# phi(q) kept in DRAM with its 32-row blocks in their new order, and loaded in one transfer, for 22 of 32 tiles; new ranks for the list that orders the program

## The chip, the cores and the metric

One Trainium2 chip, one of its cores. The kernel runs alone on that core; the time is device time in microseconds (us) from launch to end, taken for each execution, and a version's time is the median of its runs.

## The reference

x has 2048 rows of 640 float32 numbers. Two equal layers are applied, each a linear attention block of 32 heads of 20 columns and an MLP with a squared ReLU of 1728 columns, with a layer norm before each and the input added to the output:

```python
def _A_ref(x, wqkv, wo):
    B, S, D = x.shape
    H = 32; Dh = D // H
    qkv = (x @ wqkv).reshape(B, S, 3, H, Dh).transpose(2, 0, 3, 1, 4)
    q, k, v = qkv[0], qkv[1], qkv[2]
    phi = lambda t: jnp.where(t > 0, t + 1, jnp.exp(t)) + 1e-6
    pq, pk = phi(q), phi(k)
    kv = jnp.einsum("bhsd,bhse->bhde", pk, v)
    z = jnp.einsum("bhsd->bhd", pk)
    num = jnp.einsum("bhqd,bhde->bhqe", pq, kv)
    den = jnp.einsum("bhqd,bhd->bhq", pq, z)[..., None] + 1e-6
    return (num / den).transpose(0, 2, 1, 3).reshape(B, S, D) @ wo
def _B_ref(x, w1, b1, w2, b2):
    h = jnp.einsum("bsd,df->bsf", x, w1) + b1
    r = jnp.where(h > 0, h, 0)
    return jnp.einsum("bsf,fd->bsd", r * r, w2) + b2
x = A_x
for layer in range(2):
    x = x + _A_ref(_layernorm(x), A_wqkv, A_wo)
    x = x + _B_ref(_layernorm(x), B_w1, B_b1, B_w2, B_b2)
```

## The kernel before

**Tiles and stages.** The rows are 16 tiles of 128 (t = 0 to 15), in four groups of four. Every float32 matrix product is made of three matmul passes, from operands that are split into a high and a low part. A layer has three stages. *Stage A* makes k and q of all tiles, phi of both, and gathers kv and z (the sum of phi(k)). phi(q) of a tile, 128 x 640, is written to a DRAM buffer `pqd[t]` by SP (L1075 and L1159), since kv is known only when all tiles are through. For six tiles of each layer, `LATE` (9, 11, 12, 13, 14, 15 in layer 0 and 8, 9, 11, 13, 14, 15 in layer 1), q is made later, in a *bridge* between the stages, and stored at L1190, the last of them (tile 15) at L2194 in `late_line`. The bridge makes M (kv times wo) and starts the first unit of the MLP. The *group stage* then runs the attention output and the MLP of the four groups, interleaved.

**phi(q) on its way back.** `b_load_pq` (L839) loads a tile as `pqt`. Its 4 x 4 blocks of 32 rows and 160 columns change places on the way, so that the later transposes of 32 x 32 blocks come out right: a tile comes in four transfers of 32 x 4 x 160 numbers (L842), each from pieces of 160 numbers (640 bytes) in DRAM. `b_ops` (L849) works on it on DVE in four steps: `pr` = pqt times z (L853), the sum per head `den` (L860), its reciprocal and pqt times it (L866, L867, L869), and the transpose to `z` (L874). `p_split` on ACT and DVE makes the matmul operand `pT` of it.

**Pairs.** Two tiles together get their attention output in seven products (class `Pair`: p1, p2, p4, p6, p7, p5, p3) on PE, which all use the PSUM bank `po0`. After each, ACT or DVE reads the bank, in DVE's case with the adds of L1913 (`uu`, `su`, `xr`), and only then can PE start the next product.

**MLP.** The first product goes by units in Strassen's manner (PE L1584, adds L1616 and L1626 on DVE), the second is PE L1733. Their weights are kept in DRAM as `kept_w...` and come through a ring of buffers `u` by SP's loads at L572, each of which waits until PE has freed a buffer.

**What sets the order.** The program is scheduled by hand: each engine runs its instructions in the order in which they were written. For the group stage a planner (classes `Line` and `Clock`) sets that order while the program is built. Generators, called lines (`q_line` with the load of pqt and b_ops, `pair_line`, `fc1_line`, `fc2_line`, `ring_line`, `late_line` and others), yield steps such as `"SP", cost, call`, and `Clock` keeps an estimated time for each engine. Of the lines whose next step could go on an engine, the one with the smallest key goes first: its time less `early`, then its rank. `RANK` (L60) holds a pair (rank, early) for each kind of line, layer and group, and `at`, the times at which ACT, DVE and other engines are taken to be free as the stage begins. In a step for SP a number is the cost of one transfer, and a tuple that of four (`n = 4 if isinstance(us, tuple) else 1`). SP's queue holds all loads and stores in one order; each waits there for its buffer or its data.

Of the kernel before, what the change touches and what calls it, by code (L numbers as in the profile page):

```python
# [23 lines left out]
B32 = 32  # L24
# [34 lines left out]

RANK = (  # L60
    dict(
        full=((4, 0.0), (5, 0.0), (4, 0.0), (9, 0.4)),
        half=((5, 0.8), (5, 0.8), (5, 0.8), (5, 0.8)),
        moves=((8, 0.0), (4, 0.0), (5, 0.8), (9, 0.2)),
        unit=((2, 0.0), (2, 0.0), (2, 0.2), (0, -0.5)),
        next=((5, 0.8), (5, 0.8), (5, 0.8), (5, 0.8)),
        preset=((1, 0.0), (0, 0.8), (2, 0.2), (2, 0.2)),
        strip=((9, 0.0), (9, -0.2), (2, -0.2), (2, -0.2)),
        bias=((4, 0.0), (3, 0.2), (3, 0.2), (3, 0.0)),
        fc1=((4, -0.2), (1, -0.2), (1, -0.2), (2, -0.2)),  # L70
        fc2=((6, 0.0), (8, 0.0), (6, 0.0), (6, 0.0)),
        q0=((5, 0.0), (5, 0.0), (3, 0.0), (2, 0.8)),
        q1=((6, 0.0), (6, 0.0), (6, 0.0), (2, 0.0)),
        pair=((2, 0.0), (0, 0.0), (0, -0.2), (0, 0.2)),
        load_x=((5, 0.0), (5, 0.0), (5, 0.0), (5, 0.0)),
        x0=((5, 0.0), (9, 0.0), (9, -0.5), (9, -0.5)),
        x1=((9, 0.0), (4, 0.0), (4, 0.0), (4, 0.0)),
        t=((1, 0.2), (2, 0.2), (5, 0.4), (4, 0.0)),
        x1_load=((9, -0.2), (6, -0.2), (6, -0.2), (6, -0.2)),
        late=((4, 0.8), (4, 0.8), (9, 0.8), (9, 0.8)),  # L80
        mixed=((0, 0.4), (8, 0.4), (0, 1.5), (6, 1.5)),
        ring=((0, 0.0), (2, 1.5), (7, 1.5), (0, 0.0)),
        kq=((3, 0.4), (3, 0.0), (4, 0.0), (3, 0.0)),
        at=(5.0, 5.6, 2.2, 13.3),
    ),
    dict(
        full=((0, 0.0), (0, 0.0), (0, 0.8), (0, -0.5)),
        half=((6, 0.2), (1, 0.0), (1, 0.0), (1, 0.0)),
        moves=((3, 0.0), (1, 0.8), (6, 0.8), (9, 0.0)),
        unit=((1, 0.8), (1, 0.8), (1, 0.8), (1, 1.5)),  # L90
        next=((4, -0.2), (5, -0.2), (5, -0.2), (5, 0.0)),
        preset=((7, 0.0), (9, 0.0), (1, 0.0), (4, 0.0)),
        strip=((8, 0.0), (8, 0.0), (8, 0.0), (8, 0.0)),
        bias=((9, -0.2), (8, -0.5), (2, -0.5), (3, 0.0)),
        fc1=((5, 0.0), (0, 0.0), (3, 0.0), (2, 0.0)),
        fc2=((6, 0.4), (3, 0.4), (3, 0.4), (7, 0.4)),
        q0=((9, 0.0), (2, 0.0), (0, 0.0), (4, 0.0)),
        q1=((6, 0.0), (6, 0.0), (6, 0.0), (2, 0.0)),
        pair=((0, 0.0), (2, 0.0), (2, 0.0), (4, 0.0)),
        load_x=((7, 0.4), (7, 0.4), (7, 0.4), (7, 0.4)),  # L100
        x0=((5, 0.0), (9, 0.2), (3, 0.0), (5, 0.0)),
        x1=((9, 0.0), (6, 0.0), (8, -0.2), (8, -0.2)),
        t=((7, -0.5), (7, -0.2), (2, -0.2), (1, 0.4)),
        x1_load=((0, 0.4), (0, 0.4), (0, 0.4), (0, 0.4)),
        late=((9, 0.2), (2, 0.2), (2, 0.4), (0, 0.0)),
        mixed=((3, 0.0), (9, 0.0), (0, 0.0), (0, 0.0)),
        ring=((2, 0.0), (2, 0.0), (7, 0.0), (2, 0.0)),
        kq=((5, -0.5), (5, -0.5), (5, -0.5), (5, 0.4)),
        at=(4.8, 3.8, 1.5, 19.7),
    ),  # L110
)
T_FIRST = "0 u0 2 0 v0 2 u0 2 u2 v0 2 v2 u2 v2"
# [179 lines left out]
def kernel(  # L292
# [405 lines left out]
    for layer in range(N_LAYERS):  # L698
# [138 lines left out]
        def b_load_pq(t):  # L837
            if t < NT:
                pq[t] = ftile("pqt")  # L839
                v = pqd[t].rearrange("(i q) (j r) -> j q i r", i=JB, j=JB)  # L840
                for j in range(JB):
                    nc.sync.dma_start(  # L842
                        pq[t][j * B32 : (j + 1) * B32].rearrange("q (i r) -> q i r", i=JB), v[j]
                    )

        def b_load_x(t):
            xr[t] = ftile("xr")
# [123 lines left out]
        for t in range(NT):  # L971
# [15 lines left out]
            if first:  # L987
# [197 lines left out]
        def late_rest(n=9):  # L1185
            for _ in range(min(n, len(late_todo))):
                t, j = late_todo.pop(0)
                late_phi[t].rest()
                if j == 1:
                    nc.sync.dma_start(pqd[t], late_phi.pop(t).r)  # L1190

        late_q(1)
        if layer == 0:
# [785 lines left out]
        def q_line(t, first, after):  # L1979
# [209 lines left out]
        def late_line():  # L2189
            t = late_todo[-1][0]  # L2190
            for n in range(2):
                yield "DVE", 2 * cost("DVE", HD), lambda: late_phi[t].rest(1)
            yield "made", "late"
            yield "SP", MB, lambda: nc.sync.dma_start(pqd[t], late_phi[t].r)  # L2194
            yield "end f", 1
            yield "end f", 1, "got"

# [201 lines left out]
```

## Time and profile before

| what | us |
|---|---|
| median of three runs | 1330.86 |
| the runs | 1327.1, 1330.92, 1330.86 |
| the profiled execution | 1328.1 |
| span of the profiled execution | 1326.3 |
| PE busy | 1315.4 |
| DVE busy | 978.9 |
| ACT busy | 774.3 |

The page's times are those of one execution; the span runs from its first instruction to its last. An engine's busy time is the sum over its instructions. Transfers are listed by their issues: of the 128 loads of pqt (80 KB each) the median from issue to landing was 5.6 us, of the stores from stage A (320 KB) 2.3 us. A name such as "DVE pr L853 <- DMA pqt<-pq" in a list of waits reads: DVE, about to write pr at line 853, waited for the transfer that fills pqt from pq.

### The profile page before, as it was taken

The page shows a single profiled execution, that of the slowest core. Times are in us where ns is not written, and L with a number is a line of the kernel's source. Part 1 is how long each engine was busy: PE and PEld are TensorE (multiplying, and loading weights), DVE is VectorE, ACT ScalarE, POOL GpSimd, SP SyncE. Part 2 cuts the span into 40 slices and gives each one's busy share as a digit, 9 for nine tenths or more (in the row PEclk, how much of TensorE's full clock was granted, in tenths as well). Part 3 has the DMA queues.
Part 4 walks back from the last instruction along what each step waited for, and adds up shares of the span by engine and source line. Part 5 has one row for each costly group of instructions (what it writes and reads, how often), then busy time and mean ns, then how long its engine had stood idle before and what let it go on. Part 6 is the DMA issues. An engine that isn't in the chain of part 4 may idle for free.

```text
span 1326.3 us, 21333 instructions
## 1 busy us (share of the span) xinstructions
PE 1315.4 (99%) x7616; PEld 1177.2 (89%) x7616; DVE 978.9 (74%) x1923; ACT 774.3 (58%) x1760; POOL 145.5 (11%) x194
## 2 busy tenths in 40 slices
PE   9999999999999999999999999999999999999999
PEld 8888899989889889888888899998998898898887
DVE  8989988899887786552467678799978887765323
ACT  5988865745665645642757687557364744654422
POOL 1343410000000000000112132000000000000000
PEclk9999999999999999999999999999999999999999
DMA  6679876496878868799821114276877888687775
GB/s 209 226 273 342 319 241 190 146 331 218 284 256 325 282 206 295 264 351 360 276 100 42 59 40 126 58 213 202 283 254 237 281 299 271 222 297 262 275 284 177
DMA packets 118656, 310.86 MB, mean 234 GB/s; under 512 B 14934, under 2 KB 40150, under 8 KB 118518
## 3 DMA queue, kind: packets, MB, share of 16 engines
q1 hardware_dynamic: 117038, 306.81, 67.9%
q10 hardware_dynamic: 1512, 2.69, 0.7%
q8 instruction: 60, 0.98, 0.3%
q14 instruction: 46, 0.38, 0.1%
HBM read 248.66 MB, written 62.23 MB: 234 GB/s over the span
## 4 chain that ended last, share of the span: by engine, by line
PE 93%; DVE 3%; DMA 2%; ACT 1%; issue 1%; POOL 0%; SPq 0%; DVEq 0%; ACTq 0%; POOLq 0%
PE PS L643 35%; PE PS L1733 27%; PE PS L1584 17%; PE PS L1594 5%; PE PS L1550 3%; PE PS L664 3%; PE PS L1261 1%; PE PS L1290 1%; PE PS L997 1%; DMA pqt<-pq 1%; DMA st<-in_B_w_dram 1%; DMA u<-kept_wG 1%; DMA u<-kept_w 0%; ACT z L631 0%; PE PS L793 0%
## 5 line engine op out<-in xcount | busy, mean ns | idle before, releaser
L1733 PE MATMUL PS<-u,h 128*128 128x512 f32 x1318 | 342.2, 391 | 2.0 <-DMA u<-kept_w 2.0
L631 ACT ACTIVATE z<-y 32x160 f32<-32x160 f32 x774 | 258.5, 334 | 66.3 <-DVE y L618 55.5
L643 PE MATMUL PS<-kq,xT 128*128 128x320 f32 (+2 forms) x1575 | 282.1, 334 | 0.2 <-DVE GT L785 0.2
L1733 PEld LDWEIGHTS PS<-u,h 128*128 128x128 f32 x1318 | 238.9, 188 | 45.8 <-ACT uT L2202 1.7
L643 PEld LDWEIGHTS PS<-kq,xT 128*128 128x128 f32 x1575 | 250.2, 188 | 25.7 <-issue 1.0
L1584 PE MATMUL PS<-tx,u 128*128 128x256 f32 x1152 | 161.5, 283 | 1.0 <-ACT s L1606 0.8
L1584 PEld LDWEIGHTS PS<-tx,u 128*128 128x128 f32 x1152 | 151.0, 191 | 4.8 <-ACT s L1606 1.0
L1662 ACT ACTIVATE hr<-PS,b1sb 128x512 f32<-128x512 f32 x104 | 71.4, 686 | 127.4 <-PE PS L1594 103.2
L1584 PEld LDWEIGHTS PS<-xTb,u 128*128 128x128 f32 x864 | 121.4, 190 | 10.9 <-ACT PS L1612 1.0
L1584 PE MATMUL PS<-xTb,u 128*128 128x256 f32 x864 | 126.4, 282 | 0.5 <-ACT PS L1612 0.5
L598 POOL TENSOR_SCALAR rs<-mv 128x1 f32<-128x1 f32 x62 | 32.9, 531 | 847.7 <-DVE mv L595 847.7
L643 PE MATMUL PS<-kh,xh 128*128 128x512 f32 x480 | 124.5, 392 | 0.1
L1668 DVE TENSOR_TENSOR hr<-hr 128x512 f32<-128x512 f32 x73 | 49.8, 688 | 69.5 <-ACT h L1681 69.3
L643 PEld LDWEIGHTS PS<-kh,xh 128*128 128x128 f32 x480 | 87.0, 188 | 15.1 <-DVE kh L935 0.5
L746 ACT ACTIVATE e<-PS 128x320 f32<-128x320 f32 (+4 forms) x128 | 53.3, 435 | 76.9 <-PE PS L643 70.0
L1733 PE MATMUL PS<-h,u 128*128 128x512 f32 x328 | 93.2, 392 | 0.0
L1681 ACT ACTIVATE h<-hr 128x512 fp32r<-128x512 f32 x104 | 64.6, 629 | 38.2 <-PE PS L1733 36.7
L1594 PE MATMUL PS<-xTb,u 128*128 128x512 f32 x288 | 79.1, 393 | 0.0
L754 DVE TENSOR_SCALAR e<-e 128x320 f32<-128x320 f32 (+4 forms) x128 | 41.7, 326 | 50.6 <-ACT e L746 50.3
L1671 DVE TENSOR_TENSOR h<-hr,h 128x512 fp32r<-128x512 f32 x104 | 70.5, 684 | 8.2 <-ACT hr L1666 5.4
L1733 PEld LDWEIGHTS PS<-h,u 128*128 128x128 f32 x328 | 59.8, 188 | 11.2 <-ACT h L1681 0.2
L1616 DVE TENSOR_TENSOR PS<-PS,s 128x256 f32<-128x256 f32 x48 | 20.8, 433 | 63.0 <-ACT PS L1612 63.0
(172 smaller groups left out, 1906.2 us busy)
## 6 DMA issues: line engine op xcount, KB each, us to landing
u<-kept_w SPq DMA_DIRECT2D x116, 640.0 KB, 5.4
u<-kept_wE SPq DMA_DIRECT2D x48, 512.0 KB, 4.4
u<-kept_wH SPq DMA_DIRECT2D x48, 512.0 KB, 4.9
u<-kept_wG SPq DMA_DIRECT2D x48, 512.0 KB, 4.4
u<-kept_wF SPq DMA_DIRECT2D x48, 512.0 KB, 5.4
x<-x SPq DMA_DIRECT2D x40, 320.0 KB, 5.4
pqt<-pq SPq DMA_DIRECT2D x128, 80.0 KB, 5.6
st<-in_B_w_dram SPq DMA_DIRECT2D x26, 320.0 KB, 4.9
```

The lines of the kernel that those rows point to most:

```text
L631: nc.scalar.activation(d, v, AF.Copy)
L643: nc.tensor.matmul(ps, a, b, start=first and i == 0, stop=last and i == 2)
L664: nc.tensor.matmul(ps[:, j * 512 : j * 512 + HD], aT[:, k, c, :], w[c][:, l, j * HD : (j + 1) * HD], start=c == 0 and i == 0, stop=c == DC ...
L746: nc.scalar.activation(self.e[:, a:b], ps, AF.Exp)
L754: nc.vector.tensor_scalar(e, e, 1.0, PHI_EPS, op0=ALU.min, op1=ALU.add)
L1584: nc.tensor.matmul(ps, l[:, d], r[:, d], start=start and d == 0 and n == 0, stop=d == 1 and n == 2, skip_group_check=True,)
L1594: nc.tensor.matmul(ps, l[:, k], r, start=False, stop=n == 2, skip_group_check=True)
L1662: nc.scalar.activation(r, ps, AF.Relu, bias=b1sb[:, c : c + 1])
L1668: nc.vector.tensor_tensor(out=r, in0=r, in1=r, op=ALU.mult)
L1671: nc.vector.tensor_tensor(out=h[:, 1], in0=r, in1=h[:, 0].bitcast(F32), op=ALU.subtract)
L1681: yield "ACT", cost("ACT", GT), lambda: nc.scalar.activation(h[:, 0], r, AF.Square)
L1733: nc.tensor.matmul(ps, l, r, start=(first or new) and k == 0, stop=end and k == len(a) - 1, **loose)
```

## The change

A function `stored_turned(t)` is true for all tiles of layer 1 and for the six late tiles of layer 0, 22 of 32. Such a tile is written to DRAM with its blocks already in the new order, in four stores (`q_store`), and comes back in one load of 128 x 640. The other ten tiles are stored in one transfer and loaded in four, as before. The planner is told so: the load of a turned tile costs one transfer, the store of `late_line` four. The rank tables of both layers are replaced.

```diff
@@ RANK, layer 0 (two of its 23 rows)
-        pair=((2, 0.0), (0, 0.0), (0, -0.2), (0, 0.2)),
+        pair=((1, 0.0), (3, 0.0), (1, 0.0), (1, 0.0)),
...
-        at=(5.0, 5.6, 2.2, 13.3),
+        at=(4.8, 5.1, 2.9, 13.8),
@@ def b_load_pq(t):
             if t < NT:
                 pq[t] = ftile("pqt")
+                if stored_turned(t):
+                    nc.sync.dma_start(pq[t], pqd[t])
+                    return
                 v = pqd[t].rearrange("(i q) (j r) -> j q i r", i=JB, j=JB)
                 for j in range(JB):
                     nc.sync.dma_start(
                         pq[t][j * B32 : (j + 1) * B32].rearrange("q (i r) -> q i r", i=JB), v[j]
                     )
 
+        def stored_turned(t):
+            return layer > 0 or t in LATE[layer]
+
+        def q_store(t, r):
+
+            if not stored_turned(t):
+                nc.sync.dma_start(pqd[t], r)
+                return
+            v = pqd[t].rearrange("(j q) (i r) -> i q j r", i=JB, j=JB)
+            for i in range(JB):
+                nc.sync.dma_start(v[i], r[i * B32 : (i + 1) * B32].rearrange("q (j r) -> q j r", j=JB))
@@ stage A, tile 0
-                nc.sync.dma_start(pqd[0], fq.r)
+                q_store(0, fq.r)
@@ stage A, the other tiles
-                    nc.sync.dma_start(pqd[t], f.r)
+                    q_store(t, f.r)
@@ late q
-                    nc.sync.dma_start(pqd[t], late_phi.pop(t).r)
+                    q_store(t, late_phi.pop(t).r)
@@ def q_line(t, first, after):
-                yield "SP", (MB / 0.75,), lambda: b_load_pq(t)
+                yield "SP", MB if stored_turned(t) else (MB / 0.75,), lambda: b_load_pq(t)
@@ def late_line():
-            yield "SP", MB, lambda: nc.sync.dma_start(pqd[t], late_phi[t].r)
+            yield "SP", (MB / 0.75,), lambda: q_store(t, late_phi[t].r)
```

What lies behind the inserted functions has its line number raised by 15: L853 is now L868, L1913 is L1928, L1584 is L1599. A load of a turned tile is L841, its stores are L859, and a store in one transfer is L855.

The order of the instructions moves in the group stages. Three places follow. In the rows, a name with <- is a destination and its sources, and x4 means four such instructions in a row. The first is SP in the bridge of layer 1, where the late tiles 13 to 15 are stored (`rl`) and tile 5 is loaded. Before:

```order
L1190 DMA pq_13_7343<-rl 128x640
L1190 DMA pq_14_7344<-rl 128x640
L572 DMA u<-kept_wH_780 128x1024
L842 DMA pqt<-pq_5_7335 32x4x160 x4
L572 DMA u<-kept_wG_782 128x1024
L572 DMA u<-kept_wF_637 128x1024
L2194 DMA pq_15_7345<-rl 128x640
```

And SP at the same place with the change:

```order
L859 DMA pq_13_7343<-rl 32x4x160 x4
L859 DMA pq_14_7344<-rl 32x4x160 x4
L572 DMA u<-kept_wH_780 128x1024
L841 DMA pqt<-pq_5_7335 128x640
L572 DMA u<-kept_wG_782 128x1024
L572 DMA u<-kept_wF_637 128x1024
L859 DMA pq_15_7345<-rl 32x4x160 x4
```

The order is the same; three stores are four instructions each, the load is one.

The second place is DVE in layer 0, with the block of b_ops of one of the last tiles and the pair adds of tiles 12 and 13. Before:

```order
L853 TENSOR_TENSOR pr<-pqt,zbc 128x640
L860 TENSOR_REDUCE den<-pr 128x32
L866 TENSOR_SCALAR den<-den 128x32
L867 RECIPROCAL den<-den 128x32
L869 TENSOR_TENSOR pqt<-pqt,den 128x640
L874 STREAM_TRANSPOSE z<-pqt 128x640
L1913 TENSOR_TENSOR uu<-PS,uu 128x320
L1913 TENSOR_TENSOR xr<-uu,xr 128x640
```

DVE at that pair with the change:

```order
L1928 TENSOR_TENSOR xr<-PS,xr 128x320
L868 TENSOR_TENSOR pr<-pqt,zbc 128x640
L1928 TENSOR_TENSOR uu<-PS,su 128x320
L875 TENSOR_REDUCE den<-pr 128x32
L881 TENSOR_SCALAR den<-den 128x32
L882 RECIPROCAL den<-den 128x32
L884 TENSOR_TENSOR pqt<-pqt,den 128x640
L1683 TENSOR_TENSOR hr<-hr 128x512
L1768 STREAM_TRANSPOSE strip<-PS 128x512
L1631 TENSOR_TENSOR PS<-PS,s_5457 128x256
L1804 TENSOR_TENSOR x_4888<-PS,x_4888 128x512 x2
L1928 TENSOR_TENSOR uu<-PS,uu 128x320
```

The add of p6 (uu from PS and su) has moved into the block, and the add of p7 (uu from PS and uu) stands further behind it, with work of the MLP between.

The third place is the last pairs of layer 1. DVE there before, with the block of tile 15:

```order
L853 TENSOR_TENSOR pr<-pqt,zbc 128x640
L860 TENSOR_REDUCE den<-pr 128x32
L866 TENSOR_SCALAR den<-den 128x32
L867 RECIPROCAL den<-den 128x32
L869 TENSOR_TENSOR pqt<-pqt,den 128x640
L1913 TENSOR_TENSOR su<-PS,uu 128x320
L1913 TENSOR_TENSOR xr<-PS,xr 128x320
```

DVE with the change, the block of tile 15 and the first rows of that of tile 14, which is now the later one:

```order
L868 TENSOR_TENSOR pr<-pqt,zbc 128x640
L875 TENSOR_REDUCE den<-pr 128x32
L881 TENSOR_SCALAR den<-den 128x32
L882 RECIPROCAL den<-den 128x32
L884 TENSOR_TENSOR pqt<-pqt,den 128x640
L1641 TENSOR_TENSOR PS<-PS,s_12336 128x256
L889 STREAM_TRANSPOSE z<-pqt 128x640
L1928 TENSOR_TENSOR xr<-PS,xr 128x320
L1797 TENSOR_TENSOR x_11389<-sz,x_11389 128x4x128
L868 TENSOR_TENSOR pr<-pqt,zbc 128x640
L875 TENSOR_REDUCE den<-pr 128x32
L1928 TENSOR_TENSOR uu<-PS,su 128x320
```

An add of an MLP unit (L1641) and two pair adds now stand behind the blocks. On SP, tile 15's load stands right behind the load of `kept_wF_786`, which waits for a buffer.

PE at the same place with the change runs these from the matmuls that free that buffer, in a first part:

```order
L1748 MATMUL PS<-u,h 128x512 x6
L1748 MATMUL PS<-h,u 128x512 x2
L1748 MATMUL PS<-u,h 128x512 x3
L643 MATMUL PS<-uM,pT 128x320 x6
L1599 MATMUL PS<-xTb,u 128x256 x6
L1599 MATMUL PS<-tx,u 128x256 x6
L643 MATMUL PS<-uT_9874,pT 128x320 x6
```

The second part of PE's rows follows directly:

```order
L643 MATMUL PS<-uM,pT 128x320 x3
L1599 MATMUL PS<-tx,u 128x256 x6
L1748 MATMUL PS<-u,h 128x512 x6
L1599 MATMUL PS<-xTb,u 128x256 x6
L1599 MATMUL PS<-tx,u 128x256 x12
L1748 MATMUL PS<-u,h 128x512 x3
L1748 MATMUL PS<-h,u 128x512 x3
L1599 MATMUL PS<-xTb,u 128x256 x6
```

The last of these rows is the one that works on the result of L1641; the rows ahead of it are 23 matmuls of 512 columns, 15 of 320 and 36 of 256.

More of the change, by code (lines that the diff above doesn't have):

```diff
@@ L61 @@
     dict(
[L62 to L70, printed above, removed]
@@ L80 @@
[L80 to L83, printed above, removed]
-        at=(5.0, 5.6, 2.2, 13.3),
+        full=((5, 0.0), (3, 0.0), (4, 0.0), (8, 0.8)),
+        half=((3, 0.8), (5, 0.8), (6, -0.2), (9, -0.2)),
+        moves=((6, 0.0), (1, -0.2), (5, 0.8), (2, 0.0)),
+        unit=((3, 0.0), (3, 0.0), (6, 0.0), (6, 0.2)),
+        next=((5, 0.4), (2, -0.2), (5, 0.0), (2, 0.8)),
@@ L85 @@
+        x0=((5, 0.0), (7, 0.0), (9, -0.5), (8, -0.2)),
+        x1=((9, 0.0), (4, 0.0), (4, -0.2), (4, -0.2)),
+        t=((1, 0.2), (3, 0.4), (3, -0.2), (2, 0.2)),
+        x1_load=((9, 0.0), (9, 0.4), (4, -0.2), (4, -0.2)),
+        late=((5, 0.8), (5, -0.2), (5, -0.2), (5, -0.2)),
+        mixed=((7, 0.4), (8, -0.2), (6, 0.4), (6, 0.4)),
+        ring=((0, 0.2), (0, 0.2), (0, 0.2), (0, 0.2)),
+        kq=((3, 0.0), (3, 0.0), (0, 1.5), (3, 0.0)),
+        at=(4.8, 5.1, 2.9, 13.8),
     ),
     dict(
-        full=((0, 0.0), (0, 0.0), (0, 0.8), (0, -0.5)),
@@ L106 @@
[L106 to L109, printed above, removed]
+        full=((1, 0.0), (1, 0.0), (1, 0.0), (1, 0.0)),
+        half=((6, 0.2), (0, -0.2), (4, 0.0), (1, 0.0)),
+        moves=((7, 0.8), (3, 0.4), (2, 0.4), (2, 0.8)),
+        unit=((7, 0.0), (3, 0.8), (7, 0.0), (3, 0.0)),
+        next=((2, 0.0), (5, 0.0), (2, 0.0), (2, -0.5)),
+        preset=((5, 1.5), (5, 1.5), (5, 1.5), (5, 1.5)),
@@ new lines @@
+        strip=((1, 0.4), (8, 0.0), (4, 0.0), (6, 1.5)),
+        bias=((6, -0.2), (5, 0.8), (5, 0.8), (5, 0.8)),
+        fc1=((3, 0.0), (0, 0.0), (3, 0.0), (3, 0.0)),
+        fc2=((8, 1.5), (7, 0.0), (6, 0.0), (9, 0.2)),
+        q0=((9, 0.0), (1, 0.0), (9, 0.0), (9, 1.5)),
+        q1=((9, 0.0), (5, 1.5), (5, 1.5), (5, 1.5)),
+        pair=((5, 0.0), (5, 0.0), (0, 0.0), (0, 0.0)),
+        load_x=((0, 0.0), (5, 0.4), (5, 0.4), (5, 0.4)),
+        x0=((2, 0.0), (2, 0.0), (2, 0.0), (2, 0.0)),
@@ L110 @@
+        x1=((9, 0.0), (9, 0.0), (9, 0.0), (9, 0.0)),
+        t=((0, -0.5), (2, 1.5), (2, 1.5), (2, 1.5)),
+        x1_load=((2, 0.8), (7, 0.2), (7, 0.2), (7, 0.2)),
+        late=((9, 0.2), (1, 0.2), (1, 0.8), (1, 0.4)),
+        mixed=((6, 0.0), (6, 0.0), (6, 0.0), (6, 0.0)),
+        ring=((3, 0.0), (3, 0.0), (3, 0.0), (3, 0.0)),
+        kq=((0, 1.5), (9, -0.5), (7, -0.5), (7, 0.2)),
+        at=(4.8, 3.8, 0.0, 22.7),
     ),
```

34 lines of the change are left out of this document (8 added, 26 removed).

## The prediction

> **What bounds the kernel now.** I read the page's first lines first, then its summary of the chain that ended last.
>
> ```profile
> span 1326.3 us, 21333 instructions
> PE 1315.4 (99%) x7616; PEld 1177.2 (89%) x7616; DVE 978.9 (74%) x1923; ACT 774.3 (58%) x1760; POOL 145.5 (11%) x194
> PE 93%; DVE 3%; DMA 2%; ACT 1%; issue 1%; POOL 0%; SPq 0%; DVEq 0%; ACTq 0%; POOLq 0%
> ```
>
> TensorE is busy for 1315.4 of 1326.3 us. The change leaves the number of matmuls alone, so it can only win or lose time in which PE waits. Where that time lies is shown by busy time per stage (columns: window, length, then PE, PEld, DVE, ACT and POOL busy with counts, granted clock, DMA share, GB/s). The six windows are stage A of layer 0, its first unit, its group stage, then the same three of layer 1.
>
> ```profile
> 0.00:196.00 196.00, 193.65 (x1039) 170.21 (x1040) 172.44 (x335) 152.81 (x360) 63.48 (x78) 1.00 0.79 270
> 196.00:262.00 66.00, 64.67 (x449) 62.15 (x448) 57.27 (x118) 41.47 (x90) 4.03 (x8) 1.00 0.54 163
> 262.00:667.00 405.00, 403.84 (x2346) 359.91 (x2346) 282.66 (x555) 218.47 (x486) 17.50 (x33) 1.00 0.82 284
> 667.00:855.00 188.00, 188.00 (x1015) 166.04 (x1014) 137.53 (x270) 124.75 (x310) 43.72 (x43) 1.00 0.25 75
> 855.00:932.00 77.00, 74.97 (x499) 70.48 (x498) 68.50 (x137) 46.48 (x98) 4.03 (x8) 1.00 0.63 194
> 932.00:1326.30 394.30, 390.31 (x2279) 348.43 (x2277) 260.46 (x512) 190.30 (x420) 12.73 (x24) 1.00 0.76 261
> ```
>
> PE's idle time is 2.35, 1.33, 1.16, 0, 2.03 and 3.99 us. Little is left to take: in the two group stages, where the order changes, 1.16 us and, in the second, the 3.99 us with the tail after the last matmul in it. The clock was 1.00 throughout, so no stage is slow for that. Next, who ended PE's waits (total us, times, longest), and DVE's waits for the tensor that the change touches:
>
> ```profile
> PE PS L1733 <- DMA u<-kept_w: 2.0, 2, 1.5
> PE PS L643 <- DVE xr L1913: 0.9, 1, 0.9
> PE PS L643 <- DVE uu L1913: 0.9, 1, 0.9
> PE PS L1584 <- ACT s L1606: 0.8, 1, 0.8
> DVE pr L853 <- DMA pqt<-pq: 4.2, 4, 1.8
> ```
>
> PE never waits for pqt itself. DVE does, four times, and the two PE waits of 0.9 us for DVE's L1913 stand behind two of those. So the whole visible prize of a faster pqt load is some 1.8 us. The chance of a larger effect, either way, lies in the new rank tables.
>
> **Part 1: the load in one transfer.** Place A is tile 15 of layer 1. The rows are SP's four issues, the last piece's landing as the chain has it, DVE's product pr, its next add on the chain, and the matmul that waits:
>
> ```profile
> 1110.98 2.28 SPq L842 DMA_DIRECT2D pqt<-pq  x4
> 1112.76 8.16 DMA pqt<-pq
> 1121.04 0.82 DVE L853 TENSOR_TENSOR pr<-pqt,zbc 128x640 f32<-128x640 f32 x1 [1.35 <-DMA pqt<-pq]
> 1124.18 0.40 DVE su L1913
> 1124.58 0.41 DVE xr L1913
> 1125.04 1.59 PE L643 MATMUL PS<-uM,pT 128*128 128x320 f32 x9 [0.95 <-DVE xr L1913]
> ```
>
> The piece that lands last was issued 1112.76 − 1110.98 = 1.78 us after the first. One transfer is issued where the first piece was, so if it takes the same 8.16 us from issue to landing, DVE starts 1.35 us earlier (all of its wait, since 1.78 is more) and PE's 0.95 us go: **−0.95**, with 0.40 us of DVE's gain left over. From below: if one transfer of 320 KB takes 1.78 us longer than a piece of 80 KB, nothing is won (0).
>
> Place B is the same pair of tiles in layer 0, tiles 14 and 15, which are among the six turned there:
>
> ```profile
> 456.29 2.83 SPq L842 DMA_DIRECT2D pqt<-pq  x4
> 464.98 0.83 DVE L853 TENSOR_TENSOR pr<-pqt,zbc 128x640 f32<-128x640 f32 x1 [1.84 <-DMA pqt<-pq]
> 475.52 0.45 DVE L1913 TENSOR_TENSOR uu<-PS,uu 128x320 f32<-128x320 f32 x1
> 476.02 1.15 PE L643 MATMUL PS<-uT,uS 128*128 128x320 f32 x6 [0.86 <-DVE uu L1913]
> ```
>
> DVE lost 1.84 us at 464.98, worked without a further wait for a pqt, and came to uu too late by 0.86. In the new order one block of L868 to L884 stands ahead of this uu, with another pair add inside it. With four issues in 2.83 us there, one issue saves up to that; I take **−0.86**. From below 0, if the new order makes uu wait for something else.
>
> **Part 2: the new order at the same pair (C).** In layer 1's new order the block of tile 15 (L868 to L884) stands ahead of the add L1641, whose result a unit of the MLP's first product on PE needs, and SP issues that load right behind a weight load that waits for a free buffer. So the load cannot start early, and what DVE has queued behind pr waits with it: L1641, the transpose of z, a pair add and the block of tile 14. PE's rate comes from three long rows of the chain of waits, and a landing is known for pieces and for whole 320 KB tiles in the last stage:
>
> ```profile
> 655.97 10.88 PE PS L1733 x48
> 221.43 13.20 PE PS L664 x90
> 375.62 2.15 PE PS L1584 x18
> DMA to landing us min/median/max: 3.9/6.0/8.8
> x<-x SPq DMA_DIRECT2D x12, 320.0 KB, 5.4
> xr<-x SPq DMA_DIRECT2D x10, 320.0 KB, 6.2
> ```
>
> One matmul takes 10.88/48 = 0.227 us at 512 columns, 13.20/90 = 0.147 at 320, 2.15/18 = 0.119 at 256. From the matmul that frees the weight buffer to the one that needs L1641 the new order has 23, 15 and 36 of these: 5.21 + 2.20 + 4.30 = 11.7 us. Against that stands DVE's work after the landing, 1124.18 − 1121.04 = 3.14 us for the block plus some 0.4 for L1641 (it takes as long as su's 0.40), and some 0.5 us (my estimate from SP's single issues of 0.32 to 0.36 below) from the release to the issue. So the landing must come within 11.7 − 3.14 − 0.4 − 0.5 = 7.7 us of the issue. The median row says 6.0, the 320 KB rows 5.4 and 6.2, the worst piece 8.8: spare 1.5 to 2.3, or short by 1.1. I take **+0.4** (bounds 0 and 1.5, the latter from 1.1 plus 0.4 for the two pair adds that stand behind and have little spare either).
>
> The Trainium skill (DMA: Bandwidth & Descriptors, section "Anatomy of one DMA — SWDGE (gpsimd) path") gives a transfer a fixed 2.0 us or so plus its bytes over 436 GB/s; for 320 KB that is an estimate of 2.75 us, C would cost 0, and the whole sum would be 0.4 us lower. The trace differs: 5.4 and 6.2 us, with the transfer engines 0.76 busy in that stage, so the measurement decides.
>
> **Part 3: the bridge, where late tiles are stored (D).** A turned store is four issues instead of one, and SP is in order. In layer 1 the first unit of the MLP stands right behind:
>
> ```profile
> 898.47 6.23 SPq L1190 DMA_DIRECT2D pq<-rl  x2
> 904.81 0.36 SPq L572 DMA_DIRECT2D u<-kept_wH  x1
> 905.27 2.03 SPq L842 DMA_DIRECT2D pqt<-pq  x4
> 913.47 0.32 SPq L2194 DMA_DIRECT2D pq<-rl  x1
> 913.89 0.86 SPq L848 DMA_DIRECT2D xr<-x  x2
> 917.54 0.32 SPq L572 DMA_DIRECT2D u<-kept_w  x1
> 912.63 0.88 PE L1584 MATMUL PS<-tx,u 128*128 128x256 f32 x6
> u<-kept_wH SPq DMA_DIRECT2D x2, 512.0 KB, 4.2
> 922.79 2.14 PE L1733 MATMUL PS<-u,h 128*128 128x512 f32 x8 [0.50 <-DMA u<-kept_w]
> 928.34 2.30 PE L1733 MATMUL PS<-u,h 128*128 128x512 f32 x9 [1.53 <-DMA u<-kept_w]
> ```
>
> Three more issues cost between 3 × 0.32 = 1.0 us (the single store's row) and 2.83 − 0.32 = 2.5 us (the slowest four above). The first of the two L1190 stores has cover: SP then sits until the second tile is ready, most of the 6.23 us. The second store delays kept_wH from 904.81 to 905.8 to 907.3; with 4.2 us to land that is 910.0 to 911.5, and PE needs it at 912.63. Cover is left, 1.1 us at least; without it the delay would fall on PE in full, at most 2.5. The pqt load behind it shrinks from 2.03 to some 0.34, which gives 1.7 back before the next weights. The store at 913.47 delays two xr loads within SP's idle time from 914.75 to 917.54 (2.8 us). The waits of 0.50 and 1.53 us stay: those weight loads are issued when a buffer comes free, not when SP does. Layer 0 has the same sequence, with fewer loads turned. For more transfers alongside the weights I take **+0.2** (bounds 0 and 1.0, an extra store's issue landing on PE).
>
> **Part 4: what costs nothing.** The ten turned stores of layer 1's stage A add three issues each, 10 to 25 us of SP time over 188 us in which transfers are 0.25 busy and PE 188.00 busy; this order is the same as before, and nothing PE waits for is queued there. The turned loads outside A, B and the bridge take 1.7 to 2.5 us of SP time off each; SP waits for buffers there anyway, so it is 0 except at A and B. The whole program issues as many transfers as before: 32 stores and 128 loads become 10 + 88 and 40 + 22, 160 either way; bytes are equal. Ten tiles of layer 0 keep the quarters. The other rank rows only reorder the same work among themselves; their net is 0 in my sum, with the rivals as its bounds.
>
> **The sum.** −0.95 − 0.86 + 0.4 + 0.2 = −1.2 us. The profiled execution took 1328.1 us, 1.8 more than its span, and 1326.9 follows for one like it. The three timed runs were 1327.1, 1330.92 and 1330.86, median 1330.86; the four executions shown have a mean of 1329.25. A new median will fall somewhere among such runs, so I subtract from that mean: **1328.0 us**. With the terms at their ends (A and B at 0, C 1.5, D 1.0: +2.5; C and D at 0: −1.8) and the same mean it would be 1327.4 to 1331.8; one run may also be 2 us beside that mean.
>
> **Rivals.** *The waits only change places.* One transfer of 320 KB lands no sooner than four of 80 KB (6.2 and 5.4 against 6.0 above), and the order puts something else behind. Then A and B are not won, or won and lost again: 1329.3, no change. For it: the landing rows are nearly alike. Against it: the last of four pieces was issued 1.78 us late.
>
> *Blocked DVE: slower.* In the new order DVE stands at pr with what PE needs queued behind. It decides when a load lands more than 7.7 us after issue (part 2). If two in five of the 15 turned loads of the group stages (nine of layer 1, six of layer 0) did so, each costing the 0.95 us of place A, 6 × 0.95 = 5.7 us would be added, and 1335.0 follows. For it: rows reach 8.8, and PE has no other slack. Against it: medians of 6.0 and a chance to issue earlier elsewhere; only four of 32 loads were waited for before.
>
> *More is won at the bridge.* If the weight loads behind 0.50 and 1.53 us were held by SP, after all, then the 1.7 us given back reach both, and C costs nothing: −0.95 − 0.86 − 2.0 = −3.8, so 1325.4. For it: both waits are for loads issued just behind the changed ones. Against it: SP idles ahead of the issue at 917.54.
>
> *The turned store arrives late.* A wait of b_ops for its own store, four scattered pieces instead of one, would show in the bridge alone; it is in D's upper bound.
>
> **How the numbers follow.** The forecast gets 0.38 (own range 1326 to 1332), waits that change places 0.15, blocked DVE 0.23, the bridge 0.24. A measurement of this kernel tells 0.3% from no change, 4.0 us: faster is below 1326.9, slower above 1334.9. The forecast falls faster in 0.06 of its 0.38 and the bridge in 0.24 nearly always: 0.30. Blocked DVE falls slower in 0.22 of its 0.23. The rest, 0.48, is no change. The range must hold both signs: 1323.5 (the bridge, less 2 us of spread) to 1336.0 (blocked DVE plus 1).
>
> **What would show it.** Right: no PE wait for DVE's pair adds (now L1928) near 476 and 1125, DVE's waits for pqt below 2 us in all, the bridge waits for kept_w near 2.0 as before, group stages of 404 and 393 us. C wrong: a PE wait for L1641's result, or a pr with over 1 us of waiting in front. D wrong: a wait for kept_wH, or a first unit of layer 1 above 78 us. Blocked DVE: several PE waits for L1928 of about 1 us, each behind a pr that waited. If the group stages change by over 3 us without such rows, the new order acts in a way that I have not found, and my reasons are wrong whatever the time.

## The result and the profile after

The change takes 1326.21 us (median of 22 runs, 1324.44 to 1328.07) against 1329.22 before (22 runs, 1325.31 to 1333.18): ratio 0.9977, 95% interval 0.9969 to 0.9984, so 3.0 us less. Measured again beside other kernels on one chip it came to 1324.72 against 1328.25: 0.9968 (0.9955 to 0.9982). Both lie about at the 0.3% that the prediction called the limit of what can be told; with 22 runs on each side the gain itself is clear of noise. The runs also lie closer together: they spread over 3.6 us instead of 7.9. The shortest times differ by only 0.9 us (1324.44 and 1325.31), so the gain is larger in the longer executions.

The first lines of the page of the profiled execution after:

```profile
span 1323.2 us, 21315 instructions
PE 1314.5 (99%) x7616; PEld 1176.8 (89%) x7616; DVE 970.0 (73%) x1910; ACT 779.7 (59%) x1773; POOL 146.5 (11%) x194
```

PE is busy 0.9 us less and the span is 3.1 us shorter: what went is mostly PE's idle time. The new ranks also give work to another engine: 13 instructions have gone from DVE to ACT (1923 to 1910, 1760 to 1773). The waits of PE after, and DVE's for the loaded tile (total us, times, longest):

```profile
PE PS L1748 <- DMA u<-kept_w: 1.6, 2, 1.2
PE PS L793 <- POOL ident masks.py:199: 1.4, 1, 1.4
PE PS L1599 <- ACT s L1621: 0.8, 1, 0.8
PE PS L643 <- DVE r L755: 0.6, 1, 0.6
PE PS L1599 <- ACT PS L1627: 0.5, 1, 0.5
PE PS L1599 <- ACT hr L1677: 0.2, 1, 0.2
DVE pr L868 <- DMA pqt<-pq: 2.5, 3, 1.8
```

The two waits of 0.9 us for DVE's pair adds are gone; those of 1.4, 0.8, 0.6 and 0.5 us were there before as well. New is 0.2 us for ACT. DVE still waits for a pqt three times, 2.5 us in all against 4.2 (the prediction's sign was below 2), and PE stands behind the longest of these, in the group stage of layer 0:

```profile
419.98 0.43 SPq L841 DMA_DIRECT2D pqt<-pq  x1
426.40 0.83 DVE L868 TENSOR_TENSOR pr<-pqt,zbc 128x640 f32<-128x640 f32 x1 [1.80 <-DMA pqt<-pq]
431.83 0.98 PE L1599 MATMUL PS<-xTb,u 128*128 128x256 f32 x6 [0.25 <-ACT hr L1677]
```

DVE's z comes late, ACT waits 1.88 us for it before it makes pT, and its next instruction (hr, L1677) is the one that PE needs. In the traces of this order PE waits here when DVE waited 1.80 us or more (0.25, 0.35 and 1.06 us for 1.80, 1.91 and 2.61), and not at all where DVE waited 1.30 us or less.

Where the 3.1 us went can be read from the start of the same matmul (counted from the first) in both traces, at points where both orders have the same instruction. Worked out from the two traces, in us:

```
point                               before     after   difference
in the first unit of layer 0        264.40    264.29     -0.11
stage A of layer 1, early           681.24    680.32     -0.91
first unit of layer 1               914.31    913.40     -0.91
behind its second kept_w wait       928.34    926.93     -1.41
last matmul                        1322.98   1319.86     -3.12
```

The group stage of layer 0 gave 0.8 us, stage A of layer 1 nothing, the bridge 0.5 and the group stage of layer 1 1.7. In layer 0 some 0.5 us of what was won is lost again at 432 us, at the wait shown above.

### The profile page after: what moved, and what is told of

Read it like the earlier page. It is cut to its first block, busy times and chain, and to the rows that moved or that the text cites. A ratio compares the mean times of both kernels' runs of the same rounds, so it can differ in the third digit from the quotient of the medians.

```text
span 1323.2 us, 21315 instructions
## 1 busy us (share of the span) xinstructions
PE 1314.5 (99%) x7616; PEld 1176.8 (89%) x7616; DVE 970.0 (73%) x1910; ACT 779.7 (59%) x1773; POOL 146.5 (11%) x194
## 4 chain that ended last, share of the span: by engine, by line
PE 94%; DVE 2%; DMA 2%; issue 1%; ACT 1%; SPq 0%; POOL 0%; DVEq 0%; ACTq 0%; POOLq 0%
PE PS L643 35%; PE PS L1748 27%; PE PS L1599 18%; PE PS L1609 5%; PE PS L1565 3%; PE PS L664 3%; PE PS L1276 1%; PE PS L1305 1%; PE PS L1012 1%; DMA kept_w<-uprep 0%; DMA pqt<-pq 0%; DMA u<-kept_w 0%; DVE uprep L473 0%; DMA x<-x 0%; PE PS L612 0%
## 5 line engine op out<-in xcount | busy, mean ns | idle before, releaser
L1599 PE MATMUL PS<-tx,u 128*128 128x256 f32 x1152 | 161.7, 283 | 0.8 <-ACT s L1621 0.8
L1599 PEld LDWEIGHTS PS<-tx,u 128*128 128x128 f32 x1152 | 150.9, 191 | 5.1 <-ACT s L1621 1.0
L1677 ACT ACTIVATE hr<-PS,b1sb 128x512 f32<-128x512 f32 x104 | 71.2, 685 | 131.0 <-PE PS L1609 115.3
L1599 PEld LDWEIGHTS PS<-xTb,u 128*128 128x128 f32 x864 | 121.2, 190 | 10.9 <-ACT PS L1627 1.0
L1599 PE MATMUL PS<-xTb,u 128*128 128x256 f32 x864 | 126.5, 282 | 0.8 <-ACT PS L1627 0.5
L1683 DVE TENSOR_TENSOR hr<-hr 128x512 f32<-128x512 f32 x63 | 42.9, 687 | 69.8 <-ACT h L1696 69.6
L1631 DVE TENSOR_TENSOR PS<-PS,s 128x256 f32<-128x256 f32 x48 | 20.8, 433 | 68.9 <-ACT PS L1627 68.9
```

The source lines that it names most:

```text
L1599: nc.tensor.matmul(ps, l[:, d], r[:, d], start=start and d == 0 and n == 0, stop=d == 1 and n == 2, skip_group_check=True,)
L1677: nc.scalar.activation(r, ps, AF.Relu, bias=b1sb[:, c : c + 1])
L1683: nc.vector.tensor_tensor(out=r, in0=r, in1=r, op=ALU.mult)
```

## The experiments

Twelve measurements were made: of eight further kernels, and once more of the change and of three of the eight. All keep the matmuls; where the order is called the same, the planner is told the costs that belong to that order, and PE, DVE, ACT and POOL run the same instructions in the same order, and only SP's transfers differ. Times are medians in us; ratios are to the kernel before on the same chip. A ratio is the one on record with its interval; the quotient of the two medians beside it differs from it by up to 0.0005.

| kernel | time | before | ratio | 95% interval |
|---|---|---|---|---|
| new form, old order | 1326.92 | 1328.14 | 0.9987 | 0.9976 to 0.9998 |
| old form, new order | 1328.99 | 1328.14 | 1.0011 | 0.9999 to 1.0022 |
| all 32 tiles turned | 1325.13 | 1328.14 | 0.9982 | 0.9973 to 0.9992 |
| layer 1 turned only | 1327.38 | 1328.14 | 0.9992 | 0.9981 to 1.0003 |
| last pair in quarters | 1327.17 | 1328.82 | 0.9990 | 0.9979 to 1.0000 |
| four row blocks | 1327.65 | 1328.82 | 0.9992 | 0.9979 to 1.0004 |
| one store, one load | 1325.01 | 1328.82 | 0.9973 | 0.9960 to 0.9986 |
| sixteen stores | 1327.55 | 1328.82 | 0.9991 | 0.9977 to 1.0005 |
| the change again | 1324.72 | 1328.25 | 0.9968 | 0.9955 to 0.9982 |
| new form, old order, again | 1326.37 | 1328.25 | 0.9987 | 0.9976 to 0.9998 |
| all 32 tiles turned, again | 1324.95 | 1328.25 | 0.9972 | 0.9962 to 0.9983 |
| four row blocks, again | 1327.90 | 1328.25 | 0.9995 | 0.9983 to 1.0006 |

**Form and order apart.** The first two kernels split the change into its halves: the transfers alone, and the order alone.

```diff
 new form, old order (against the change)
-RANK of the change
+RANK of before
-                yield "SP", MB if stored_turned(t) else (MB / 0.75,), lambda: b_load_pq(t)
+                yield "SP", (MB / 0.75,), lambda: b_load_pq(t)
-            yield "SP", (MB / 0.75,), lambda: q_store(t, late_phi[t].r)
+            yield "SP", MB, lambda: q_store(t, late_phi[t].r)
```

> The new store and load form alone, in the order of before on PE, DVE, ACT and POOL (old ranks, planner told the old costs). Theory 'the form': the two PE waits of 0.9 us for the pair adds (near 476 and 1125 us) go and the bridge waits for kept_w shrink by some 0.4, so about 2.2 us less than before, ratio 0.9983, and no PE wait for DVE's pair adds left. Rival 'the order': the gain sits in the new ranks, so the time equals before (ratio 0.9995 to 1.0005) even if single waits move.

```diff
 old form, new order (against the change; the planner is told the change's costs)
         def stored_turned(t):
-            return layer > 0 or t in LATE[layer]
+            return False
```

> The new order on PE, DVE, ACT and POOL with all tiles stored in one transfer and loaded in four quarters, as before. Theory 'the form': at most 1 us less than before (ratio 0.9992 to 1.000), with DVE's waits for pqt back at 4 us or more. Rival 'the order': as fast as the change, ratio 0.9977. Third: the order is fitted to single loads, and with quarters DVE's chains behind pr come late, ratio 1.001 or more.

The form alone gave 0.9987, some 1.7 us, in both measurements (1.2 and 1.9 by the medians). The order alone gave nothing: 1.0011, if anything slower. Together they gave 0.9977 and 0.9968. So in the new order the form is worth 0.0034 of the ratio, about 4.5 us (1.0011 to 0.9977; 3.9 by the medians), two to three times what it is worth in the old one. It was the third expectation for the order that held: the order goes with single loads.

The places show why. In the old order with the new form, SP's issues and DVE's pr for tile 15 of layer 1 (A) and tile 14 of layer 0 (B), from the timeline:

```profile
1110.83 0.51 SPq L841 DMA_DIRECT2D pqt<-pq  x1
1119.66 0.82 DVE L868 TENSOR_TENSOR pr<-pqt,zbc 128x640 f32<-128x640 f32 x1
456.72 0.38 SPq L841 DMA_DIRECT2D pqt<-pq  x1
463.60 0.82 DVE L868 TENSOR_TENSOR pr<-pqt,zbc 128x640 f32<-128x640 f32 x1
```

At A the issue came at the same time as the first of four before (1110.83 and 1110.98), yet DVE began 1.4 us sooner and with no wait ahead of it; at B 1.4 us sooner too, though that execution was 0.4 us behind there. Against before, the matmuls behind come 1.22 us earlier at A and 1.12 at B, by the difference of the two traces there, and again 1.22 and 1.12 in the second run of this kernel. The waits of 0.95 and 0.86 us were these. The expectation that no wait for a pair add would be left did not hold: at 294 us PE waits 0.6 us for one in the first trace of this kernel and 0.9 in the second, behind a tile of layer 0 that comes in four as before.

In the new order with the old form, the timeline at the last pair of layer 1 (place C), SP's issues, DVE and the two matmuls that wait:

```profile
1137.67 2.38 SPq L845 DMA_DIRECT2D pqt<-pq  x4
1146.32 0.83 DVE L871 TENSOR_TENSOR pr<-pqt,zbc 128x640 f32<-128x640 f32 x1 [1.26 <-DMA pqt<-pq]
1149.38 0.43 DVE L1644 TENSOR_TENSOR PS<-PS,s 128x256 f32<-128x256 f32 x1
1149.86 0.98 PE L1602 MATMUL PS<-xTb,u 128*128 128x256 f32 x6 [0.80 <-DVE PS L1644]
1152.80 0.82 DVE L871 TENSOR_TENSOR pr<-pqt,zbc 128x640 f32<-128x640 f32 x1 [1.28 <-DMA pqt<-pq]
1154.93 1.14 PE L643 MATMUL PS<-uT,uS 128*128 128x320 f32 x6 [1.14 <-DVE uu L1931]
```

And in the change at the same place:

```profile
1134.58 0.42 SPq L841 DMA_DIRECT2D pqt<-pq  x1
1141.54 0.43 DVE L1631 TENSOR_TENSOR PS<-PS,s 128x256 f32<-128x256 f32 x1 [2.52 <-ACT PS L1627]
1142.00 0.83 DVE L868 TENSOR_TENSOR pr<-pqt,zbc 128x640 f32<-128x640 f32 x1
1145.06 0.42 DVE L1641 TENSOR_TENSOR PS<-PS,s 128x256 f32<-128x256 f32 x1
```

With quarters each load is 1.3 us late for DVE, and PE stands 0.80 us for the MLP add (now L1644, three lines lower) and 1.14 for the pair add. With one load DVE does not wait for it: the trace has its landing 6.4 us after the issue, at 1140.94, and DVE comes to pr 1.1 us later, when it has made an add (L1631) for which it waited for ACT. L1641 ends at 1145.48, and PE needs it at 1145.80, 0.3 us later. So in this execution the load could have come 1.4 us later before PE had stood, and the last 0.3 us are left by ACT and DVE, not by the load.

**How far turning should go.** Two kernels change only the set of turned tiles.

```diff
 all 32 tiles turned
-            return layer > 0 or t in LATE[layer]
+            return True
 layer 1 turned only
-            return layer > 0 or t in LATE[layer]
+            return layer > 0
```

> The change with the other ten tiles of layer 0 turned too (tiles 0 to 8 and 10), same order. Four stores instead of one, ten times, fall into stage A of layer 0, where transfers are 0.79 busy and SP also carries the weight loads. Theory 'issues are hidden': stage A unchanged, time as the change, ratio to before 0.9977. Rival 'SP is full there': weight loads behind the stores come 1 to 2.5 us later each time, stage A or the bridge of layer 0 grows by 1 us or more, ratio 0.9985 or above.

> The change with the six late tiles of layer 0 back in one store and four loads, same order; layer 1 stays turned. Theory 'the form': the wait at the pair of tiles 12 and 13 of layer 0 comes back in part, some 0.9 us more than the change, ratio to before 0.9984. Rival 'the order': as the change, 0.9977, because the new order has moved the pair add away from the loads.

> All 32 tiles turned, in the change's order. Theory 'issues are hidden and single loads help': as the change or up to 1 us less, since DVE's wait of 1.8 us at 426 us, for a tile of layer 0, and PE's gap of 0.5 us at 432 behind it are gone. Rival 'stage A pays': 0.5 us or more slower than the change.

With all tiles turned, the second measurement beside the change on one chip was 1324.95 against 1324.72: no difference. Its ten stores of four issues in stage A of layer 0 are hidden; the same matmul there starts within 0.25 us of the change's up to the group stage. The gain that was hoped for from the ten tiles was not seen either, and it could not come from there: the load that DVE waits for at 426 us is L841 in the change, so its tile was turned already. With layer 1 alone the ratio is 0.9992, so the six late tiles of layer 0 look to be worth a good half of the gain (the intervals, 0.9981 to 1.0003 and 0.9969 to 0.9984, just overlap). That is about twice what was expected, and mostly at another place. Against the change the trace loses 0.6 us at 355 us, with a wait of 0.3 for a pair add, and 1.25 at 447 (a further 2.0 at 922 lies in the bridge, where its transfers are the change's and the wait for kept_w varies anyway). At 447 it is no pqt that PE waits for. SP's two issues in the change, then the same two and PE in the kernel with layer 1 alone:

```profile
438.92 0.38 SPq L841 DMA_DIRECT2D pqt<-pq  x1
441.32 0.32 SPq L572 DMA_DIRECT2D u<-kept_wG  x1
...
438.92 1.95 SPq L845 DMA_DIRECT2D pqt<-pq  x4
441.33 0.34 SPq L572 DMA_DIRECT2D u<-kept_wG  x1
448.55 0.95 PE L1602 MATMUL PS<-tx,u 128*128 128x256 f32 x6 [1.00 <-DMA u<-kept_wG]
```

The weights kept_wG are issued at the same time, 441.32 and 441.33. In the change PE runs the matmul that needs them at 447.38 without a wait, so they were there by then; behind four transfers they land 7.1 us after their issue, and PE loses 1.0. In the old form, new order, they took 6.4 us at this place and PE waited 0.35; of the two executions with four row blocks here one has 0.1 us of this wait and the other none. Of the six other executions with one load here (the change again, both runs of all tiles turned, the last pair, one store, sixteen stores) none has it. So a load in four can delay the load behind it, though SP issues that one in time: a path that the prediction did not have. It shows in three of four traces, with 0.1 to 1.0 us.

**The last pair alone.** The mechanism at C was then tried by itself.

```diff
-            return layer > 0 or t in LATE[layer]
+            return (layer > 0 and t < 14) or (layer == 0 and t in LATE[layer])
```

> The change with only tiles 14 and 15 of layer 1 back in one store and four loads; same order. Theory 'late last piece': at the last pair of layer 1 DVE waits about 1.3 us at pr for each of the two tiles and PE then waits about 0.8 for the MLP add behind the first and 1.1 for the pair add behind the second; the last stage grows by 2 us and the rest stays: ratio to before 0.9992. Rival 'what happens earlier moves it' (the delays of the other quarter loads set that place): no PE wait there, ratio 0.9977.

The ratio, 0.9990, is what was expected, but the profiled execution shows only a small part: DVE's waits at pr were 0.23 and 0.39 us, the wait for the MLP add did not come, and the one for the pair add was 0.2. The profiled execution was the fastest of the twelve (1324.69); the median was 1327.17. So one profile is not the median. That the load comes later in the longer executions is likely (1.3 us of waiting in the old form's, against 0.23 and 0.39 here), but no trace of this kernel shows it.

**Issues or piece size.** One load in place of four differs in two ways: the number of issues, and pieces of 2,560 bytes in DRAM for pieces of 640. A turned tile loaded in four row blocks has the large pieces and four issues.

```diff
-                    nc.sync.dma_start(pq[t], pqd[t])
+                    for j in range(JB):
+                        s = slice(j * B32, (j + 1) * B32)
+                        nc.sync.dma_start(pq[t][s], pqd[t][s])
```

> The change, with each turned tile's load cut in four by rows (4 x 32 rows of 640 numbers, pieces of 2,560 bytes) in place of one. Theory 'issues': what counts is that SP spends about 2 us on four issues and the last piece comes late, so as with quarters, ratio 1.0011, with waits for pqt of 6 us or more on DVE. Rival 'pieces': what counts is the piece of 640 bytes against 2,560, so as the change, ratio 0.9977.

> Turned tiles loaded in four row blocks, in the change's order. Theory 'issues': clearly slower than the change on the same chip, by 0.001 to 0.002 of the ratio, as in the first run (0.9992). Rival 'pieces': equal to the change within 0.0005.

> The change itself, beside the three below on one chip, so that small differences can be read between them. Expected from the first measurement: ratio to before 0.9977, waits of PE for pair adds none.

> The new form in the old order once more. Theory 'the order adds': 0.001 of the ratio slower than the change on the same chip (0.9987 against 0.9977), since the old order keeps a short wait at its own pairs. Rival 'only the form counts': equal to the change within 0.0005.

On one chip the row blocks took 1327.90 against the change's 1324.72: 3.2 us of the gain is gone when only the load is cut in four. DVE's waits for a tile, in the row blocks of the first and the second run and then in the old form, all in the new order:

```profile
DVE pr L873 <- DMA pqt<-pq: 7.2, 7, 2.1
...
DVE pr L873 <- DMA pqt<-pq: 9.3, 9, 2.7
...
DVE pr L871 <- DMA pqt<-pq: 9.4, 9, 2.6
```

DVE waits about as long with the large pieces as with the small ones. What that costs differs: the first profile is the fastest of its twelve runs (1324.47), and PE waits 0.4 us behind these loads at C; the second is that of a run of 1329.91. The landing tells the rest. These rows (transfers, bytes each, median us from issue to landing) are, in turn, before and the change with the transfer engines mostly idle (700 to 845 us, some 0.25 busy), before in the last stage, and the change in the last stage:

```profile
xt<-x SPq DMA_DIRECT2D x9, 320.0 KB, 3.0
pq<-r SPq DMA_DIRECT2D x8, 320.0 KB, 2.3
pqt<-pq SPq DMA_DIRECT2D x12, 80.0 KB, 2.3
...
pqt<-pq SPq DMA_DIRECT2D x3, 320.0 KB, 3.3
...
pqt<-pq SPq DMA_DIRECT2D x36, 80.0 KB, 6.0
...
pqt<-pq SPq DMA_DIRECT2D x9, 320.0 KB, 6.4
```

The second row is a store, the others are loads. The traces have the landing of only some transfers: of the last two rows 17 of 36 and 3 of 9. With idle engines a whole tile takes 0.7 to 1.0 us longer than a quarter of it (3.0 and 3.3 against 2.3 us); in the last stage it lands about as fast (6.4 against 6.0 us), so there a tile in four comes later by about what SP needs for the other three issues: 2.38 us less one issue in the rows at C. The Trainium skill has a rule for two transfers to separate halves of the partitions (DMA: Bandwidth & Descriptors, "Rules for kernel authors"): they run on the same engines, so one transfer over 128 partitions should be used. The runs agree for four parts: in the last stage a quarter landed only 0.4 us sooner than a whole tile, and the four row blocks, which are such parts, cost 3.2 us. The row blocks change two things, however, the number of issues and the 32 partitions of each; a load in four that spans all partitions was not tried. The busy time of the transfer engines differs as well. The group stage of layer 0 in the change and then in the row blocks (the last but one number is the share of time that the transfer engines are busy, the last GB/s):

```profile
262.00:667.00 405.00, 404.75 (x2350) 360.41 (x2350) 279.27 (x548) 221.75 (x495) 18.20 (x33) 1.00 0.80 284
262.00:667.00 405.00, 403.95 (x2340) 358.90 (x2339) 277.83 (x546) 220.33 (x491) 18.26 (x33) 1.00 0.82 284
```

At the same 284 GB/s they are busy for 0.80 with one load for each turned tile, and for 0.82 with four row blocks, as before the change; no run shows what that costs. Whether the piece size adds something to the time is not settled: the row blocks' 0.9992 and 0.9995 stand against 1.0011 for the quarters, but the intervals meet.

The change and the old order with the new form, measured together, stand at 1324.72 and 1326.37: with single loads the new order is worth about 1.7 us (the intervals of the two ratios overlap, 0.9955 to 0.9982 and 0.9976 to 0.9998). Their profiles do not put it in one place. The second run of the old order has the 0.9 us for a pair add at 294 us and 0.4 for a kept_wG at 1073; the first run had 0.6 at 294 and nothing at 1073. The wait at 294 is not the order's: PE runs the same instructions there in both orders, and the old form in the new order has it too, with 0.5 us. Which places carry the order's part stays open.

**The stores.** One kernel removes the three extra issues of each turned store (and with them the new order of the blocks), another adds twelve to one store.

```diff
 one store, one load (the blocks stay in the old order)
-            if not stored_turned(t):
+            if not stored_turned(t) or layer >= 0:
                 nc.sync.dma_start(pqd[t], r)
                 return
 sixteen stores (layer 1, tile 14 only: n = 4, w = 8; elsewhere n = 1, w = 32)
             for i in range(JB):
-                nc.sync.dma_start(v[i], r[i * B32 : (i + 1) * B32].rearrange("q (j r) -> q j r", j=JB))
+                for m in range(n):
+                    nc.sync.dma_start(
+                        v[i][m * w : (m + 1) * w],
+                        r[i * B32 + m * w : i * B32 + (m + 1) * w].rearrange("q (j r) -> q j r", j=JB),
+                    )
```

> The change, with the 22 tiles stored in one transfer and loaded in one, so that the blocks are not brought into their new order (left out). Three issues less per store, 66 in all. Theory 'stores are hidden': as the change, ratio 0.9977. Rival 'stores cost': the bridge or stage A gets shorter, 0.5 us or more less than the change, ratio 0.9973 or below.

> The change with tile 14 of layer 1 stored in sixteen transfers instead of four, right ahead of kept_wH in the bridge. Twelve more issues at 0.4 to 0.5 us are 5 to 6 us; kept_wH was issued at 905.27 in the change, lands 4.2 later, and PE needs it at 911.7, so 2.2 us of cover. Theory 'cover': PE waits 2.8 to 4 us for kept_wH and the time grows by that, ratio to before 0.9998 to 1.0007. Rival 'not through SP': the load is not held, no wait for kept_wH, ratio 0.9977.

Without the extra issues the ratio was 0.9973 (0.9960 to 0.9986), beside 0.9977 and 0.9968 for the change: the 66 issues cost nothing that can be measured. The bridge of layer 1 in the change, SP and then the two matmuls that wait there:

```profile
897.55 7.62 SPq L859 DMA_DIRECT2D pq<-rl  x8
905.27 0.38 SPq L572 DMA_DIRECT2D u<-kept_wH  x1
905.75 0.37 SPq L841 DMA_DIRECT2D pqt<-pq  x1
912.58 1.88 SPq L859 DMA_DIRECT2D pq<-rl  x4
914.56 0.87 SPq L863 DMA_DIRECT2D xr<-x  x2
916.63 0.32 SPq L572 DMA_DIRECT2D u<-kept_w  x1
...
921.74 2.14 PE L1748 MATMUL PS<-u,h 128*128 128x512 f32 x8 [0.38 <-DMA u<-kept_w]
926.93 2.29 PE L1748 MATMUL PS<-u,h 128*128 128x512 f32 x9 [1.17 <-DMA u<-kept_w]
```

Since the change runs 0.91 us ahead here, kept_wH at 905.27 is 1.37 us later than before (905.27 + 0.91 − 904.81), and kept_w at 916.63 is where it was (917.54). With sixteen stores the cover runs out:

```profile
897.06 11.31 SPq L865 DMA_DIRECT2D pq<-rl  x20
908.47 0.35 SPq L572 DMA_DIRECT2D u<-kept_wH  x1
...
912.35 0.95 PE L1608 MATMUL PS<-tx,u 128*128 128x256 f32 x6 [0.95 <-DMA u<-kept_wH]
915.70 0.95 PE L1608 MATMUL PS<-tx,u 128*128 128x256 f32 x6 [1.01 <-DMA u<-kept_wG]
```

This execution is 0.5 us ahead of the change at that point, so kept_wH goes out 3.7 us later than in the change (908.47 + 0.5 − 905.27), not 5 to 6: the twelve issues took 0.31 us each. PE loses 2.0 us to two waits (2.2 by the difference of the traces) where 2.8 to 4 for one were expected, and the ratio is 0.9991. So stores do reach PE through SP's queue, and the cover is real: of 3.7 us, 2.7 were hidden ahead of the first of the two waits (2.2 were expected).

## Why the prediction was right, and where its sizes were off

- **Direction and size.** Faster by 1.2 us was forecast, and 3.0 was measured, 0.23%, inside a range that is 12.5 us wide and holds the time before as well, so the number alone says little; the second measurement, 0.32%, is just beyond the 0.3%. 1326.21 lies at the edge of the forecast's own 1326 to 1332. The reference point, the mean 1329.25 of the four executions shown, met the median of 22 runs, 1329.22; with four runs that spread over 3.8 us that is in part luck.
- **A and B, −0.95 and −0.86.** Right, shown by the form in the old order: 1.22 and 1.12 us. That is the two waits and some 0.27 us by which the matmuls right behind each took longer (1.59 us for nine where 9 × 0.147 = 1.32, and 1.15 for six where 0.88). The premise that one transfer of 320 KB lands as soon as one of 80 KB held where it was needed, in the loaded stages (6.4 and 6.0 us, and 4.7 in the old order), not with idle engines.
- **C, +0.4.** The deadline was placed rightly: PE's matmuls from the release to the one that needs L1641 took 11.8 us in the change (1134.02 to 1145.80), forecast 11.7. The load landed 6.4 us after its issue, 1.4 us before it would have held PE, so the price was 0. The 2.75 us that the prediction worked out from a fit for the gpsimd path is not what such a load, issued by SP, took even with idle engines: 3.3 us. In quarters pr came 8.65 us after the first issue, 0.95 beyond the 7.7, and PE waited 0.80 us for L1641's result; with the 1.14 for the pair add that is above the 1.5 that was set as the upper bound of this place.
- **D, +0.2.** Right as a delay (1.37 us, forecast 1.0 to 2.5, with cover), and 0 as a price. The waits for kept_w stayed, 1.55 us against 2.03; in the other kernels' executions they lie between 0.5 and 2.3, so this 0.5 us of the profile can be chance.
- **Part 4, 0.** Right for stage A (no difference between 681 and 914 us), also when all tiles are turned. The other half, "their net is 0 in my sum" for the rest of the ranks, is the step that failed: with single loads the new order is worth about 1.7 us, and with quarters it is worth nothing or less. Form and order were added as if they were independent; by these runs they are not. Missing as well is the delay that four transfers can put on a weight load behind them (1.0 us at 447 with layer 1 alone).
- **The rivals.** Blocked DVE happened in the change once, at another place: the wait of 1.80 us at 426 and PE's 0.5 us behind it. In the old form with the new order it happens at C as well. There PE loses 2.5 us at the two late loads and 0.8 at 432, of the 5.5 us by which that trace is behind the change's; most of the rest lies at 294, 447, 973 and in the bridge. More won at the bridge did not happen: SP stands idle from 915.43 to 916.63, ahead of the issue of kept_w. That the waits only change places does not fit A and B, which were won in the change too; of B some 0.5 us went again at 432.

With A and B at their measured −2.3 and C and D at 0 the forecast's sum would be −2.3 us, and no experiment accounts for the 0.7 that is left of the 3.0 (in the one pair of profiles the bridge gives 0.5). It is not simply the order's worth: the form in the old order gained 1.2 and 1.9 us by the medians and not 2.3, and its traces lose 0.8 and 1.1 us at 294. Beside the change on one chip the two parts are 1.9 for the form and 1.7 for the order, of 3.5.

## What to carry to other kernels

A load in four pieces is complete only when its last issue has landed, and it can make the load behind it later too. Where an engine works in order behind such a load, merging the issues gains that time even if bytes and total issues stay equal, and the extra issues are best put on the side (here the store) that has cover. An instruction order belongs to the transfers that it runs with: measure the order and the form each alone before adding their gains. One profile can be the lucky one: those of the last pair in quarters and of the row blocks' first run were the fastest of twelve, 2.5 and 3.2 us below their medians, and show hardly a wait of PE for DVE.

## What was not expected of the hardware

In the last stage, with the transfer engines 0.76 busy, a load of 320 KB took about as long from issue to landing as one of 80 KB (6.4 and 6.0 us); with the engines mostly idle it took 3.0 to 3.3 us against 2.3. Four issues to turn a tile took 1.74 to 2.38 us of SP's time at C, but sixteen small ones in the bridge cost 0.31 us for each that was added. A weight load issued at the same time landed 7.1 us after its issue behind four transfers and 6.1 at most behind one; in three other executions with four it was 6.4 us or less.
